# A top-k attention and low-rank mixer kernel: the softmax division moved to a tile by features, by way of DRAM

## The chip, the cores and the metric

The kernel runs on one core of a Trainium2 chip. The metric is the device time of one execution in microseconds; the median of several runs is compared. The engines named below are PE (the matrix engine; PEld is its loading of weights), DVE (vector engine), ACT (scalar engine), POOL (GpSimd) and SP (which here only issues transfers). SPq and ACTq are the queues in which SP and ACT issue transfers.

## The reference

Attention over 8 batches and 8 heads, 576 positions, 64 features a head, with only the 32 largest scores of each row kept; then a mixer that adds a low-rank mixing of the positions (rank 32) and a two-layer perceptron over the 512 features.

```python
scores = scale * np.matmul(q, k.transpose(0, 1, 3, 2))
kth = np.partition(scores, -32, axis=-1)[..., -32:-31]
scores = np.where(scores >= kth, scores, -1000000000.0)
attn = np.exp(scores - np.max(scores, axis=-1, keepdims=True))
attn = attn / (np.sum(attn, axis=-1, keepdims=True) + 1e-09)
x = heads_side_by_side(np.matmul(attn, v))        # (batch, 576, 512)
h = x.transpose(0, 2, 1) @ U @ V                  # over positions
u = x + h.transpose(0, 2, 1)
out = u + np.maximum(u @ w_ch1, 0.0) @ w_ch2
```

All data is fp32.

## The kernel before

**Pairs, tiles, steps.** Two heads make a pair g (NPAIR = 4 pairs a batch, 32 pairs). The 576 query rows of a pair are five tiles: four of 128 rows (t = 0 to 3, both heads side by side) and a tail of 64 rows (t = NT = 4, the two heads one above the other on the 128 partitions). From the second batch on (step ALONE = 20) a step handles one tile, and the fourth step of a pair handles t = 3 and the tail together. A large loop over steps n writes out by hand in which order every engine gets its work; each engine and each transfer queue runs its list strictly in that order. Step n does the scores of step n+1's tiles, the top-k search of step n, the exponentials and turned probabilities of step n-1, and the values of steps before (`weighted`).

**One tile.** PE computes the scores (`scores`, L332, L364), ACT copies them to SBUF (L377), POOL and DVE fold them (`pair`, L428 to L431), DVE searches the largest values (`front`), ACT and POOL make the probabilities, with row sums collected in `den`, one column for each tile and head. `blocks` turns the probabilities block by block on DVE (L572), stores them in DRAM (`away`, four transfers on SP, L578), and `back` fetches them in turned order (`PT<-away`, on ACT's queue, L587). The tail is turned on PE instead (`turns`).

**Values.** `values(g, t)` multiplies by V on PE. For t < NT the result lies by features: partition = head and feature, column = query row (L646, L649); ACT copies it to `XT` (L658). For the tail it lies by positions, 5 products (L633); ACT scales it with the inverse row sums from `den` into the tail part of X (L641, twice). `inverse` turns `den` into reciprocals on DVE (L621).

**Mixing.** `mixed(g, wait, lag)` is a generator, advanced once by each `fill()` of the big loop. It turns XT on PE to lie by positions (L672, four transposes), ACT copies that to X (L676), and POOL multiplies it with the inverse row sums (L677), so the division is made on the tile by positions, where a row sum belongs to a partition. Then PE multiplies with U (L688), ACT copies to Tb (L696), and in two parts (320 and 256 columns) PE multiplies with V (L700) and adds X, turned back to lie by features, into the same PSUM tile (L702: four transposes and a product with `ident2` for the tail). ACT copies the parts to `uT` (L710). Two X tiles serve the pairs in turn.

**Filler.** Each batch's perceptron (`mlp`, L742 and L760) is cut into single products, which `fill()` deals out between the steps of the next batch's attention. `turned_back` turns its results and stores them (L784 to L795). The last batch's perceptron is written out by itself after the loop (`closing`), in an order of its own.

**SP's queue** in steps of the later batches: the transfers of `away` (they wait for DVE's L572), the loads of q for the next pair in the step with t = 0 and of k and v in the step with t = 1 (`loading`, L255 to L288), and the output stores. The k and q tiles are turned by DVE (L302) a step later.

Of the kernel before, what the change touches and what calls it, by code (L numbers as in the profile page):

```python
# [8 lines left out]
F32 = mybir.dt.float32  # L9
# [3 lines left out]
ALU = mybir.AluOpType  # L13
# [13 lines left out]
def kernel(  # L27
# [28 lines left out]
    nc = tc.nc  # L56
    B, H, S, D = q.shape
    P = 128
# [37 lines left out]
    WIDE = 2 * P + TAIL  # L96

    ident = const.tile([P, P], F32, name="ident")
# [5 lines left out]
    vds = [const.tile([P, P], F32, name=f"vd{i}") for i in range(NV)]  # L104
    vts = [const.tile([P, 2, D], F32, name=f"vt{i}") for i in range(NV)]

    xs = [const.tile([P, NT + 1, P], F32, name=f"x{i}") for i in range(2)]
    for i in range(NV):
        nc.gpsimd.memset(vds[i], 0.0)
        nc.gpsimd.memset(vts[i], 0.0)  # L110
    for x in xs:
        nc.gpsimd.memset(x[:, NT, :], 0.0)
    W1Q = F // NT
    w1s = [const.tile([P, NC, W1Q], F32, name=f"w1{i}") for i in range(NT)]
    w2 = const.tile([P, NF, C], F32, name="w2")
# [2 lines left out]
    V = const.tile([NT * R, S], F32, name="V")  # L118
# [115 lines left out]

    raw, qkTs, S2s, uTs, XTs, dens = {}, {}, {}, {}, {}, {}
    probs, PTs, folds, fronts_of = {}, {}, {}, {}
    inverted, aways = set(), {}

    def load(g):

# [318 lines left out]
    def shared(g, t):  # L559


        return t < NT and g >= ROUNDED
# [29 lines left out]
    def turns(g, t):  # L592


        if shared(g, t):
            return
        E2 = probs.pop((g, t))
        nh = 2 if t < NT else 1
        if t == NT and g >= NPAIR:
            PT = attn.tile([P, NT + 1, P], F32, tag="PTt", name="PTt", bufs=1)  # L600
        else:
            PT = attn.tile([P, 2 * NT + 1, P], F32, tag="PT", name="PT")
        PTs[g, t] = PT
# [12 lines left out]

    def inverse(g, lo, hi):
        den = dens[g][:, lo:hi]
        if g == NPAIR - 1:
            nc.vector.tensor_scalar_add(den, den, 1e-9)  # L620
        nc.vector.reciprocal(den, den)  # L621

    def values(g, t):

        PT = PTs.pop((g, t))
        va, vd, vt = (a[g % NV] for a in (vas, vds, vts))
        O = ps_t.tile([P, P], F32, tag="tp", name="O")
        if t == NT:
            den, x = dens[g], xs[g % 2]
            if g not in inverted:  # L630
                inverse(g, 2 * NT if g == NPAIR - 1 else 0, 2 * NT + 1)
            for j in range(NT + 1):
                nc.tensor.matmul(  # L633
                    O,
                    lhsT=PT[:, j],
                    rhs=va[:, :, j, :] if j < NT else vt,
                    start=(j == 0),
                    stop=(j == NT),
                )
            for h in range(2):  # L640
                nc.scalar.mul(x[half(h), NT, half(h)], O[half(h), half(h)], den[half(h), 2 * NT :])  # L641
            return
        if shared(g, t):
            PT = PT.rearrange("p c n -> p (c n)")
            PT = PT.rearrange("p (a c j) -> p c a j", a=4, j=BLK)
        nc.tensor.matmul(O, lhsT=vd, rhs=PT[:, 2 * NT], start=True, stop=False)  # L646
        for j in range(NT):
            for h in range(2):
                nc.tensor.matmul(  # L649
                    O[half(h)],  # L650
                    lhsT=va[:, h, j, :],
                    rhs=PT[:, NT * h + j],
                    start=False,
                    stop=(j == NT - 1),
                )
        if t == 0:
            XTs[g] = attn.tile([P, MAIN], F32, tag="XT", name="XT", bufs=1)
        nc.scalar.copy(XTs[g][:, cols(t)], O)  # L658


    def mixed(g, wait, lag=0):

        for _ in range(lag):
            yield
        b, gi = divmod(g, NPAIR)
        if gi == 0:
            uTs[b] = mlpp.tile([P, NC, S], F32, tag="uT", name="uT")
        XT, den = XTs.pop(g), dens[g]
        X = xs[g % 2]
        tp = ps_t.tile([P, NT, P], F32, tag="tp", name="tp")  # L670
        for t in range(NT):
            nc.tensor.transpose(tp[:, t, :], XT[:, cols(t)], ident)  # L672
        X4 = X[:, 0:NT, :].rearrange("p t (h d) -> p t h d", h=2)
        tp4 = tp.rearrange("p t (h d) -> p t h d", h=2)
        den4 = den[:, 0 : 2 * NT].rearrange("p (t h) -> p t h ()", h=2).to_broadcast([P, NT, 2, D])
        nc.scalar.copy(X4, tp4)  # L676
        nc.gpsimd.tensor_tensor(X4, X4, den4, ALU.mult)  # L677
        if wait is None:
            waiting.append(g)
            while g in waiting:  # L680
                yield
        else:
            for _ in range(wait):
                yield
        pT = ps_t.tile([P, P], F32, tag="tp", name="pT")
        for t in range(NT + 1):
            i = t % NT * R
            nc.tensor.matmul(  # L688
                pT[i : i + R, :],
                lhsT=U[:, t, :],  # L690
                rhs=X[:, t, :],
                start=(t < NT),
                stop=(0 < t),
            )
        Tb = mlpp.tile([P, P], F32, tag="Tb", name="Tb")
        nc.scalar.copy(Tb, pT)  # L696
        yield
        for chunks, (lo, hi) in zip(PARTS, SPAN):
            up = ps_t.tile([P, WIDE], F32, tag="tp", name="up")
            nc.tensor.matmul(up[:, 0 : hi - lo], lhsT=Tb, rhs=V[:, lo:hi], start=True, stop=False)  # L700
            for t in chunks:
                nc.tensor.matmul(  # L702
                    up[:, OFF[t] - lo : OFF[t] - lo + rows(t)],
                    lhsT=X[:, t, :],
                    rhs=ident if t < NT else ident2,
                    is_transpose=True if t < NT else None,
                    start=False,
                    stop=(t == chunks[-1]),
                )
            nc.scalar.copy(uTs[b][:, gi, lo:hi], up[:, 0 : hi - lo])  # L710
            yield
        if gi == NPAIR - 1:
            fillers.append(closing(b) if b == B - 1 else mlp(b))
# [371 lines left out]
    def tiles(n):  # L1085

        return steps[n] if 0 <= n < STEPS else []

    def weighted(m):

        for g, t in reversed(tiles(m)):
            values(g, t)
        if tiles(m)[-1][1] == NT:
            mixing.append(mixed(g, None, 1) if m < STEPS - 1 else mixed(g, 5, 0))
# [6 lines left out]
    def turned(n):  # L1101

        for g, t in tiles(n):
            yield from turns(g, t)
# [3 lines left out]
    t = 0  # L1108
# [5 lines left out]
    for n in range(STEPS + 2):  # L1114
        if n < STEPS:
            g, t = steps[n][0]
# [6 lines left out]
        else:  # L1123
            t = NT
# [93 lines left out]
        next_params(1)  # L1218
        fill()
        if n >= STEPS:  # L1220
            weighted(n - 2)
        elif n - 2 >= ALONE and len(tiles(n - 2)) > 1:
            g2 = steps[n - 2][0][0]
            inverted.add(g2)
            inverse(g2, 0, 2 * NT + 1)
        next(here, None)
        bound = tiles(n + 1)[:1] == [(NPAIR + 1, 0)]
        if not bound:
# [7 lines left out]
        for tile_ in tiles(n - 1):  # L1236
            if shared(*tile_):
                blocks(*tile_)
        turning = turned(n - 1)
        if n < STEPS and t < 2 and g + 1 < NP:  # L1240
            if t == 0:
                coming = loading(g + 1)
            next(coming)
# [41 lines left out]
```

## Time and profile before

| | us |
|---|---|
| median of 3 runs | 1685.63 (1685.03 to 1686.02) |
| the profiled execution | 1686.28 |
| its span, first to last instruction | 1684.5 |

Over the span PE is busy 94%, the weight loads 72%, DVE 92%, ACT 59% and POOL 56%. The transfers move 180.97 MB; SP's queue carries 257712 packets and ACT's 16032. The granted clock of PE is 0.81 in the first 260 us and 0.96 to 1.00 afterwards.

| stretch, us | PE | DVE | ACT | POOL | what |
|---|---|---|---|---|---|
| 0 to 260 | 175.13 | 247.52 | 193.33 | 178.77 | first batch, parameters |
| 260 to 380 | 119.32 | 109.40 | 85.91 | 79.95 | second batch begins |
| 380 to 456.78 | 70.09 | 76.66 | 44.00 | 42.99 | |
| 836.54 to 1026.42 | 189.88 | 185.65 | 113.65 | 105.15 | one of the repeating batches |
| 1510 to 1600 | 88.05 | 42.70 | 34.43 | 42.02 | last pair, last perceptron begins |
| 1600 to 1684.5 | 80.55 | 36.19 | 12.54 | 13.54 | last perceptron |

A row gives the busy time of each engine in the stretch. An engine whose busy time equals the length of the stretch never rests there.

### The profile page before, as it was taken

The page shows a single profiled execution, that of the slowest core. Times are in us where ns is not written, and L with a number is a line of the kernel's source. Part 1 is how long each engine was busy: PE and PEld are TensorE (multiplying, and loading weights), DVE is VectorE, ACT ScalarE, POOL GpSimd, SP SyncE. Part 2 cuts the span into 40 slices and gives each one's busy share as a digit, 9 for nine tenths or more (in the row PEclk, how much of TensorE's full clock was granted, in tenths as well). Part 3 has the DMA queues.
Part 4 walks back from the last instruction along what each step waited for, and adds up shares of the span by engine and source line. Part 5 has one row for each costly group of instructions (what it writes and reads, how often), then busy time and mean ns, then how long its engine had stood idle before and what let it go on. Part 6 is the DMA issues. An engine that isn't in the chain of part 4 may idle for free.

```text
span 1684.5 us, 29512 instructions
## 1 busy us (share of the span) xinstructions
PE 1586.0 (94%) x9498; PEld 1213.4 (72%) x9498; DVE 1543.7 (92%) x4364; ACT 1000.1 (59%) x2475; POOL 939.0 (56%) x741
## 2 busy tenths in 40 slices
PE   4666799999899999999999999999999999999999
PEld 2444466788677887788777887778777887778876
DVE  7999998999999999999999999999999999994452
ACT  4888778665665656565665656565665656554320
POOL 4778668655555555555555555555555455552620
PEclk7788799999999999999999999999999999999999
DMA  3323232254545555554545555554545455533001
GB/s 87 96 75 96 58 91 73 55 133 123 131 110 136 125 131 128 131 129 120 128 117 130 125 130 125 132 125 125 128 115 131 122 134 124 131 105 102 10 1 29
DMA packets 273898, 180.97 MB, mean 107 GB/s; under 512 B 171376, under 2 KB 258256, under 8 KB 273744
## 3 DMA queue, kind: packets, MB, share of 16 engines
q1 hardware_dynamic: 257712, 117.49, 30.2%
q10 hardware_dynamic: 16032, 61.61, 11.7%
q8 instruction: 75, 1.23, 0.3%
q14 instruction: 79, 0.65, 0.1%
HBM read 108.23 MB, written 70.78 MB: 106 GB/s over the span
## 4 chain that ended last, share of the span: by engine, by line
PE 54%; DVE 32%; SPq 4%; DMA 4%; issue 2%; POOL 2%; ACT 1%; DVEq 0%; ACTq 0%; POOLq 0%
PE mm L760 16%; PE mm L742 16%; DVE m L516 10%; DVE upper L511 9%; PE sc L332 4%; PE O L649 4%; DVE first L498 3%; PE mm L836 3%; DVE y L572 3%; DVE upper L483 2%; PE sc L836 2%; PE tp L836 2%; DVE place L511 2%; DMA ld<-in_k_dram 2%; SPq L255 2%
## 5 line engine op out<-in xcount | busy, mean ns | idle before, releaser
L742 PE MATMUL mm<-uT,w 128*128 128x320 f32 (+1 forms) x1792 | 461.1, 410 | 1.9 <-ACT hT L755 1.9
L760 PE MATMUL mm<-hT,w 128*128 128x320 f32 (+1 forms) x1792 | 461.5, 408 | 0.0
L546 POOL TENSOR_TENSOR Ssb<-Ssb,E 128x576 f32<-128x576 f32 x243 | 339.4, 1416 | 210.7 <-ACT E L545 210.4
L742 PEld LDWEIGHTS mm<-uT,w 128*128 128x128 f32 x1792 | 333.7, 191 | 97.5 <-issue 12.0
L760 PEld LDWEIGHTS mm<-hT,w 128*128 128x128 f32 x1792 | 330.5, 190 | 90.3 <-issue 10.2
L516 DVE MAX8 m<-upper 128x8 f32<-128x304 f32 (+1 forms) x780 | 367.4, 512 | 0.7
L511 DVE MATCH_REPLACE8 upper<-m,upper 128x304 f32<-128x304 f32 (+1 forms) x520 | 259.9, 507 | 0.0
L431 POOL TENSOR_TENSOR lower<-lower,upper 128x576 uint32<-128x576 uint32 x108 | 152.3, 1410 | 157.5 <-DVE upper L430 152.6
L428 POOL TENSOR_TENSOR lower<-Ssb 128x576 uint32<-128x576 uint32 x108 | 152.4, 1411 | 144.0 <-ACT Ssb L377 87.0
L435 ACT ACTIVATE Ssb<-Ssb,nmax 128x576 f32<-128x576 f32 x258 | 200.8, 780 | 22.3 <-POOL Ssb L522 10.1
L332 PE MATMUL sc<-qkT 64*128 64x288 f32 (+1 forms) x1056 | 178.8, 460 | 10.8 <-ACT Ssb L386 7.8
L545 ACT ACTIVATE E<-Ssb,least 128x576 f32<-128x576 f32 x243 | 176.2, 768 | 4.2
L483 DVE MAX8 upper<-lower 128x8 f32<-128x288 f32 x432 | 172.2, 440 | 6.9 <-POOL lower L431 6.9
L377 ACT COPY Ssb<-sc 128x576 f32<-128x576 f32 x216 | 127.6, 643 | 69.2 <-PE sc L332 69.1
L572 DVE STREAM_TRANSPOSE y<-Ssb 128x512 f32<-128x512 f32 (+1 forms) x312 | 155.4, 547 | 8.8 <-ACT Ssb L435 8.8
L755 ACT ACTIVATE hT<-mm 128x320 f32<-128x320 f32 (+1 forms) x224 | 92.1, 411 | 112.2 <-PE mm L742 107.4
L649 PE MATMUL O<-PT,va 128*64 128x128 f32 x2048 | 145.1, 286 | 0.0
L332 PEld LDWEIGHTS sc<-qkT 64*128 64x128 f32 (+1 forms) x1056 | 95.7, 197 | 51.2 <-issue 16.4
L649 PEld LDWEIGHTS O<-PT,va 128*64 128x64 f32 x2048 | 113.8, 141 | 16.3 <-issue 1.6
L511 DVE MATCH_REPLACE8 upper<-first,upper 128x304 f32<-128x304 f32 x216 | 97.7, 460 | 0.0
L481 DVE MATCH_REPLACE8 lower<-upper,lower 128x288 f32<-128x288 f32 x216 | 94.1, 444 | 0.0
L430 DVE TENSOR_TENSOR upper<-sc,Ssb 128x576 f32<-128x576 f32 x108 | 80.3, 744 | 12.7 <-ACT Stail L397 12.4
(250 smaller groups left out, 2201.3 us busy)
## 6 DMA issues: line engine op xcount, KB each, us to landing
away<-y SPq DMA_DIRECT2D x416, 144.0 KB, 2.5
PT<-away ACTq DMA_DIRECT2D x104, 576.0 KB, 3.9
raw<-in_moe_w_ch_dram SPq DMA_DIRECT2D x32, 512.0 KB, 3.8
va<-in_v_dram SPq DMA_DIRECT2D x64, 128.0 KB, 2.6
out_dram<-ob SPq DMA_DIRECT2D x59, 128.0 KB, 2.5
ld<-in_q_dram SPq DMA_DIRECT2D x108, 64.0 KB, 3.1
ld<-in_k_dram SPq DMA_DIRECT2D x108, 64.0 KB, 2.6
ld<-in_q_dram SPq DMA_DIRECT2D x108, 8.0 KB, 3.2
```

The source lines that it names most:

```text
L332: nc.tensor.matmul(out, lhsT=qkT[half(h), 0, cols(t)], rhs=qkT[half(h), 1, lo:hi], start=True, stop=True,)
L428: nc.gpsimd.tensor_tensor(bottom, a.bitcast(U32), b.bitcast(U32), ALU.add)
L435: nc.scalar.activation(E, chunk, AF.Exp, bias=nmax, scale=SCALE, accum_out=total)
L483: nc.vector.max(spot, lower)
L511: nc.vector.match_replace(nxt, ms[c], curs[c], NEG)
L516: nc.vector.max(ms[c], curs[c])
L545: nc.scalar.activation(gap, chunk, AF.Relu, bias=least[:, c : c + 1], scale=-WIDEN)
L546: nc.gpsimd.tensor_tensor(chunk, chunk, gap, ALU.subtract)
L572: nc.vector.transpose(y[:, :, i * NT : i * NT + c].rearrange("p r c j -> p c r j"), E2[:, a : a + c * P].rearrange("p (c r j) -> p c r j", ...
L649: nc.tensor.matmul(O[half(h)], lhsT=va[:, h, j, :], rhs=PT[:, NT * h + j], start=False, stop=(j == NT - 1),)
L742: nc.tensor.matmul(ph[:, 0:w], lhsT=first_layer(cc, f), rhs=uT[:, cc, lo:hi], start=(cc == 0), stop=(cc == NC - 1),)
L760: nc.tensor.matmul(po[:, 0:w], lhsT=w2[:, f, c * P : (c + 1) * P], rhs=hTs[f][:, 0:w], start=(f == 0), stop=(f == NF - 1),)
```

## The change

For the pairs of the second batch on (g >= NPAIR):

- The reciprocals of all nine columns of `den` are stored, element by element, to a DRAM tile `rd` by six transfers on SP, right after `inverse`. A new `scale` fetches them, in feature order, as a row for each head, repeated over that head's 64 partitions: two transfers on SP, after `blocks` and ahead of the next pair's k loads. For the last pair both calls stand together in the step after the last.
- The tail's values are made by features too: ten products with 64 weight columns and 64 moving columns; one ACT copy into XT, which is now 576 columns wide. The two scaling copies L641 are gone here.
- `mixed` begins with a POOL product of XT (576 columns) and the scale row into `uT`, gives up its turn twice, and only then turns the result on PE (now with one transpose more, for the tail) and copies it to X (one ACT copy more). POOL's product with `den` (L677) is gone here.
- After the product with V there is no second turning of X (L702): ACT copies the product to a tile `mix` (one buffer), and POOL adds it to `uT`.

The first batch's pairs go on as before. There is one X tile in place of two, one Tb in place of two, and the tiles of a step that handles two are now taken with t = 3 first and the tail second.

```diff
-    xs = [const.tile([P, NT + 1, P], F32, name=f"x{i}") for i in range(2)]
+    X = const.tile([P, NT + 1, P], F32, name="x")
...
 def inverse(g, lo, hi):
         nc.vector.reciprocal(den, den)
+        if g >= NPAIR:
+            inverted.add(g)
+            rd = dram.tile([2, 2, WIDE], F32, tag="rd", name="rd")
+            scales[g] = rd
+            full = dens[g][:, 0 : 2 * NT].rearrange("p (a b h) -> p a b h", a=2, h=2)
+            for a in range(2):
+                for h in range(2):
+                    nc.sync.dma_start(
+                        rd[h, a, 0 : 2 * P].rearrange("(b p) -> p b", b=2), full[:, a, :, h]
+                    )
+            for h in range(2):
+                nc.sync.dma_start(
+                    rd[h, 0, 2 * P : WIDE].rearrange("(p o) -> p o", o=1), dens[g][half(h), 2 * NT :]
+                )
+
+    def scale(g):
+        rd = scales.pop(g)
+        sc = attn.tile([P, S], F32, tag="scale", name="scale", bufs=1)
+        scales[g] = sc
+        flat = rd.rearrange("h a n -> h (a n)")
+        for h in range(2):
+            nc.sync.dma_start(sc[half(h)], flat[h : h + 1, 0:S].to_broadcast([D, S]))
 
 def values(g, t):
         if t == NT:
+            if g >= NPAIR:
+                for j in range(NT + 1):
+                    for h in range(2):
+                        nc.tensor.matmul(
+                            O[half(h), 0:TAIL],
+                            lhsT=va[:, h, j, :] if j < NT else vt[:, h, :],
+                            rhs=PT[:, j, half(h)],
+                            start=(j == 0),
+                            stop=(j == NT),
+                        )
+                nc.scalar.copy(XTs[g][:, at(NT)], O[:, 0:TAIL])
+                return
...
 def mixed(g, wait, lag=0):
+        uT = uTs[b][:, gi]
+        if g >= NPAIR:
+            nc.gpsimd.tensor_tensor(uT, XT, scales.pop(g), ALU.mult)
+            yield
+            yield
+            XT = uT
         tp = ps_t.tile([P, NT, P], F32, tag="tp", name="tp")
         for t in range(NT):
-            nc.tensor.transpose(tp[:, t, :], XT[:, cols(t)], ident)
+            nc.tensor.transpose(tp[:, t, :], XT[:, at(t)], ident)
...
+        else:
+            if g == NPAIR:
+                nc.gpsimd.memset(X[TAIL:P, NT, :], 0.0)
+            tp = ps_t.tile([P, P], F32, tag="tp", name="tp")
+            nc.tensor.transpose(tp[0:TAIL], uT[:, at(NT)], ident)
+            nc.scalar.copy(X[0:TAIL, NT, :], tp[0:TAIL])
...
-            nc.tensor.matmul(up[:, 0 : hi - lo], lhsT=Tb, rhs=V[:, lo:hi], start=True, stop=False)
-            for t in chunks:
+            nc.tensor.matmul(
+                up[:, 0 : hi - lo], lhsT=Tb, rhs=V[:, lo:hi], start=True, stop=(g >= NPAIR)
+            )
+            for t in chunks if g < NPAIR else ():
...
-            nc.scalar.copy(uTs[b][:, gi, lo:hi], up[:, 0 : hi - lo])
+            if g < NPAIR:
+                nc.scalar.copy(uT[:, lo:hi], up[:, 0 : hi - lo])
+            else:
+                mix = attn.tile([P, WIDE], F32, tag="mix", name="mix", bufs=1)
+                nc.scalar.copy(mix[:, 0 : hi - lo], up[:, 0 : hi - lo])
+                nc.gpsimd.tensor_tensor(uT[:, lo:hi], uT[:, lo:hi], mix[:, 0 : hi - lo], ALU.add)
             yield
...
 def weighted(m):
-        for g, t in reversed(tiles(m)):
+        for g, t in tiles(m):
             values(g, t)
...
         if n >= STEPS:
+            if n == STEPS:
+                inverse(NP - 1, 0, 2 * NT + 1)
+                scale(NP - 1)
             weighted(n - 2)
         elif n - 2 >= ALONE and len(tiles(n - 2)) > 1:
-            g2 = steps[n - 2][0][0]
-            inverted.add(g2)
-            inverse(g2, 0, 2 * NT + 1)
+            inverse(steps[n - 2][0][0], 0, 2 * NT + 1)
...
         turning = turned(n - 1)
+        if n < STEPS and n - 2 >= ALONE and len(tiles(n - 2)) > 1:
+            scale(steps[n - 2][0][0])
         if n < STEPS and t < 2 and g + 1 < NP:
             if t == 0:
                 coming = loading(g + 1)
             next(coming)
```

More of the change, by code (lines that the diff above doesn't have):

```diff
@@ L110 @@
         nc.gpsimd.memset(vts[i], 0.0)
-    for x in xs:
-        nc.gpsimd.memset(x[:, NT, :], 0.0)
+    nc.gpsimd.memset(X[:, NT, :], 0.0)
     W1Q = F // NT
@@ L236 @@
     probs, PTs, folds, fronts_of = {}, {}, {}, {}
-    inverted, aways = set(), {}
+    inverted, aways, scales = set(), {}, {}
     def load(g):
@@ L628, in values @@
         if t == NT:
-            den, x = dens[g], xs[g % 2]
+            if g >= NPAIR:
[10 more added lines that the diff above has]
+                return
+            den = dens[g]
             if g not in inverted:
@@ L640, in values @@
             for h in range(2):
-                nc.scalar.mul(x[half(h), NT, half(h)], O[half(h), half(h)], den[half(h), 2 * NT :])
+                nc.scalar.mul(X[half(h), NT, half(h)], O[half(h), half(h)], den[half(h), 2 * NT :])
             return
@@ L656, in values @@
         if t == 0:
-            XTs[g] = attn.tile([P, MAIN], F32, tag="XT", name="XT", bufs=1)
-        nc.scalar.copy(XTs[g][:, cols(t)], O)
+            XTs[g] = attn.tile([P, S], F32, tag="XT", name="XT", bufs=1)
+        nc.scalar.copy(XTs[g][:, at(t)], O)
     def mixed(g, wait, lag=0):
@@ L668, in mixed @@
         XT, den = XTs.pop(g), dens[g]
-        X = xs[g % 2]
+        uT = uTs[b][:, gi]
[4 more added lines that the diff above has]
+            XT = uT
         tp = ps_t.tile([P, NT, P], F32, tag="tp", name="tp")
         for t in range(NT):
[L672 to L677, printed above, removed]
+            nc.tensor.transpose(tp[:, t, :], XT[:, at(t)], ident)
+        X4 = X[:, 0:NT, :]
+        nc.scalar.copy(X4, tp)
+        if g < NPAIR:
+            X4 = X4.rearrange("p t (h d) -> p t h d", h=2)
+            den4 = den[:, 0 : 2 * NT].rearrange("p (t h) -> p t h ()", h=2)
+            nc.gpsimd.tensor_tensor(X4, X4, den4.to_broadcast([P, NT, 2, D]), ALU.mult)
+        else:
[4 more added lines that the diff above has]
+            nc.scalar.copy(X[0:TAIL, NT, :], tp[0:TAIL])
         if wait is None:
@@ L694, in mixed @@
             )
-        Tb = mlpp.tile([P, P], F32, tag="Tb", name="Tb")
+        Tb = mlpp.tile([P, P], F32, tag="Tb", name="Tb", bufs=1)
         nc.scalar.copy(Tb, pT)
@@ L709, in mixed @@
                 )
-            nc.scalar.copy(uTs[b][:, gi, lo:hi], up[:, 0 : hi - lo])
+            if g < NPAIR:
+                nc.scalar.copy(uT[:, lo:hi], up[:, 0 : hi - lo])
[3 more added lines that the diff above has]
+                nc.gpsimd.tensor_tensor(uT[:, lo:hi], uT[:, lo:hi], mix[:, 0 : hi - lo], ALU.add)
             yield
```

## The prediction

> **What bounds the kernel now.** I read the table of stretches first. The batches repeat every 189.88 us from about 457 to 1406 us, so one such stretch, four head pairs of 47.47 us, stands for most of the span. In the lines below the columns are stretch, length, then busy time (and count) of PE, PEld, DVE, ACT, POOL, then clock, DMA share and GB/s.
>
> ```profile
> 646.66:836.54 189.88, 189.88 (x1169) 147.40 (x1169) 185.77 (x561) 113.53 (x286) 105.19 (x80) 1.00 0.51 127
> 1406.20:1510.00 103.80, 103.40 (x610) 77.31 (x610) 101.67 (x311) 61.85 (x157) 56.01 (x43) 1.00 0.50 125
> ```
>
> PE never rests; DVE rests 4.11 us in 189.88, about 1.03 us a pair. So time taken from PE's row of work is won, at most until DVE binds (1.03 us a pair), and every new wait of PE is lost in full. The chain of waits in that stretch is made of PE alone; these are its pieces for one pair (start, length, what; instructions counted; each fp32 product is two, each is_transpose one):
>
> ```profile
> 700.55 1.11 PE O L633 x10
> 701.89 1.02 PE O L649 x16
> 704.10 1.17 PE sc L332 x8
> 705.27 1.27 PE mm L760 x4
> 706.54 0.44 PE tp L672 x4
> 715.02 0.55 PE pT L688 x10
> 717.48 0.39 PE up L702 x4
> 719.43 0.22 PE up L702 x2
> ```
>
> The reader is to see the prices: 0.111 us for a 128-wide pass, 0.064 for a pass with 64 weight columns (L649), and 0.39 + 0.22 = 0.61 us a pair for the second turning of X (L702). The transposes L672 come 1.27 us after the scores, behind two products of L760.
>
> POOL and ACT at the same place, from the timeline:
>
> ```profile
> 704.83 1.18 ACT L377 COPY Ssb<-sc 128x576 f32<-128x576 f32 x2 [1.57 <-PE sc L332]
> 706.14 1.42 POOL L428 TENSOR_TENSOR lower<-Ssb 128x576 uint32<-128x576 uint32 x1 [1.90 <-issue]
> 708.06 1.04 POOL L677 TENSOR_TENSOR x<-x,den 128x512 f32<-128x512 f32 x1 [0.50 <-ACT x L676]
> 709.06 1.41 POOL L431 TENSOR_TENSOR lower<-lower,upper 128x576 uint32<-128x576 uint32 x1
> 723.05 1.41 POOL L431 TENSOR_TENSOR lower<-lower,upper 128x576 uint32<-128x576 uint32 x1 [3.19 <-DVE upper L430]
> ```
>
> POOL does the division after PE's transposes, and nothing of PE's waits for it soon: L688 comes at 715.02.
>
> Last, SP's queue and what DVE wants of it, same pair:
>
> ```profile
> 696.28 0.62 SPq L260 DMA_DIRECT2D ld<-in_q_dram  x1
> 698.29 0.41 SPq L790 DMA_DIRECT2D out_dram<-ob  x1
> 699.76 1.76 SPq L578 DMA_DIRECT2D away<-y  x4
> 701.57 0.59 SPq L255 DMA_DIRECT2D ld<-in_k_dram  x1
> 706.89 0.62 SPq L260 DMA_DIRECT2D ld<-in_k_dram  x1
> 711.13 1.38 DVE L302 STREAM_TRANSPOSE qkT<-ld 128x1152 f32<-128x1152 f32 x1 [0.91 <-DMA ld<-in_k_dram]
> ```
>
> SP issues without rest from the transposed blocks (699.76) to the end of the k loads (707.51), and DVE already waits 0.91 us for the last of them. In the other three pairs of the batch L302 does not wait, but starts within 4.5 us of the last k issue.
>
> **The change on PE.** Removed per pair: L702, 0.61 us. Added: one transpose of the 64 tail columns, 0.11 (a piece of L672). Changed: the tail's values, 5 products of 128 columns (1.11 us, L633), become 10 products with 64 weight columns and 64 moving ones, 20 passes. Bounds: at L649's 0.064 a pass 1.28 us, at half of it (half the moving columns) 0.64. I take 1.28, since L688, with 32 weight columns, still needs 0.055 a pass, so width buys little. Net: 0.61 - 0.11 - 0.17 = 0.33 us won a pair; with the other end 0.97. The columns t=NT-1 and t=NT only change places in one step.
>
> The Trainium skill, "TensorEngine Tiling (Array Packing)", Theoretical Speedup, gives up to 2x for 64 columns; by that the tail's values would be about 0.55 us (an estimate from 1.11) and the gain per pair 1.06. L649's row shows only 0.111/0.064 = 1.7x with 128 moving columns.
>
> **The new wait of PE.** The division now stands ahead of the transposes: POOL multiplies XT by the scale row into uT, and PE transposes uT. In POOL's order the product lies where L677 lay, between L428 and L431; in PE's order the transposes move back by two of the filler's turns, to about 2.6 to 2.8 us of products after the scores (five of 320 columns at 0.54, or six of 256 at 0.43). The chain from the scores' end (705.27): ACT's second copy ends 706.01, L428 runs 706.14 to 707.56, the product takes 1.41 (L546, same 128x576 form) and ends at 708.97. That is 3.70 us after the scores; the other three pairs give 3.70, 3.69 and 3.70 by the same rows. PE arrives after 2.7, so it waits 1.0 us (0.9 to 1.1). All it has queued (filler, next values and scores) waits with it, and ACT and DVE behind those. Nothing covers it, as PE has no idle time to move. Net on PE: +1.0 - 0.33 = +0.67 us a pair; with the other end of the values +0.03.
>
> Of the 32 pairs all but the four of the first batch change: 28. The last lies in the tail, and in the stretch 380 to 457 PE is busy 70.09 of 76.78, so I count 26: +17.4 us.
>
> **POOL and ACT.** POOL loses 1.04 (L677) and gains 1.41 + 0.87 + 0.74 (the additions at L772's 320 and 256 columns): +1.98 a pair on 26.3 of 47.47. The product ends where L677 ended (708.97 against 709.10), so L431 is not late there; the additions stand before the next L431, which waits 3.19 us for DVE: 1.61 fits. If that cover were gone, L431 and DVE's L483 would be up to 1.6 late. One buffer mix makes ACT's second copy wait for the first addition: POOL ends L428 at 719.02, so about 719.9, against 719.68 now: 0.2 us, up to 1.1 where a residual addition stands between; ACT then rests 5 us. ACT exchanges two L641 (0.61) for two copies of 0.26: nothing.
>
> **SP's queue.** Eight more issues a pair: six element-wise stores of the reciprocals, behind the q loads, and two broadcast loads between away and the k loads. Issue prices: four with 128 rows at 0.41 (L790), four with 64 rows at 0.53 (between L287's 0.51 and L795's 0.52 to 0.60): 3.76 us; bounds 0.37 to 0.64 each, 3.0 to 5.1. The stores fill SP's gap before away (2.0 to 2.9 us without the output stores, less with them) and push away by 0.65 to 1.1; the loads add 1.06. By these rows the k loads start 1.8 to 2.1 us later in all four pairs, provided the stores have landed by the end of away's issue. Stores of few bytes land in 1.4 to 2.5 us (out_dram rows), away's in 2.5: then nothing is added. At the 5.2 us that is the longest landing of ld, 2 to 3 us are added.
>
> What is late next is L302. With the k load's median landing of 2.6 us the extra stall is 0, 1.9, 0.5, 0 in the four pairs, mean 0.6; with 4.1, as in the pair shown, 1.3 to 1.9, mean 1.6. DVE has gained 0.67 of room by PE's wait, so 0 to 0.95 us a pair counts; both ends hang on whether k still meets the 576 KB of PT<-away, issued 705.48. I take 0.15 a pair, +3.9 us, near the lower end: shifted by 1.9, the last k load comes behind most of that transfer. The scale row itself lands about 705.7, 1.9 us before POOL wants it (707.56).
>
> The Trainium skill speaks against the stores: "DMA: Bandwidth & Descriptors", Rules for kernel authors, says a strided last dimension becomes one descriptor per element, and Specifications that under 512 B a read-modify-write is done. The trace shows 34155 packets on SP's queue taking 34.4% of 16 x 189.9 us, 30.6 ns each, most of 128 B; no row has 4 B ones. If the page's rule doubled that, the stores' 1152 packets (4 x 256 + 2 x 64) over 16 engines would take 4.4 instead of 2.2 us (an estimate), and the k loads some 1 to 2 us more: +26 to +50 us in all.
>
> **Start and tail.** The first four pairs keep their path. At the end the closing products start at 1570.3 and the last up ended at 1563.2; that 6.9 us of filler covers two turns and 1.6 us of additions: nothing, 2 us if the cover is gone.
>
> **Sum.** +17.4 + 3.9 = +21 on the profiled execution's 1686.28 (span 1684.5); that lies 0.65 above the median 1685.63, so 1707.
>
> **Rivals.**
> 1. *PE's gain without the wait (faster).* If the product is done when PE reaches the transposes, the 0.33 to 0.97 us a pair are kept, at most 1.03 (DVE): 28 x 0.5 = -14, 1672 (1658 to 1676). Place: PE before the transposes of uT; it decides once the wait there is below the gain. For it: POOL has 45% idle time. Against: the product stands behind L428, which hangs on the scores just computed. 0.17.
> 2. *DVE and SP bind.* With the upper end of the stall at L302, 0.95 counts instead of 0.15: 26 x (0.67 + 0.95) = +42, 1728 (1717 to 1750). For it: L302 waits already, and SP has no gap. Against: three of four pairs have room. 0.22.
> 3. *The stores are slow.* Landing after 5.2 us or more instead of 1.4 to 2.5 blocks SP, then k and POOL's product: +2.5 to 4 a pair, 1750 to 1790. For it: no row of such small pieces. Against: 4 KB stores land in 1.4 us. 0.06.
> 4. *No change.* Gain 0.97 against a wait of 1.0: 1686. 0.05.
>
> **How the numbers follow.** My forecast, 1695 to 1717, gets 0.50. This kernel's measurement can tell about 0.2% (3.4 us) from no change. Faster 0.17, same 0.05, slower 0.50 + 0.22 + 0.06 = 0.78. The range 1679 to 1750 leaves out nearly all of rival 1 and rival 3 and a little more, about 0.2.
>
> **What would show it.** The forecast: PE idle about 1 us before the transposes of uT, released by POOL, about 27 times, L702 gone in g>=4, PE busy below 100% in the stretches. Rival 2: DVE idle at L302 of over 1.5 us a pair on ld<-in_k. Rival 3: SP waiting for rd's landing, POOL's product waiting for a DMA. I am wrong if PE's wait there is under 0.4 us, or if the k loads start no later after y than now.

## The result and the profile after

| | us |
|---|---|
| before, median of 4 runs | 1685.66 (1685.03 to 1686.02) |
| after, median of 4 runs | 1969.03 (1962.33 to 1978.37) |
| ratio | 1.1685, 95% interval 1.1637 to 1.1734 |
| profiled execution after, its span | 1970.58, 1968.8 |

The change costs 283 us where 21 were forecast. First the chain that ended last in the kernel after, as shares of the span.

```profile
PE 39%; DVE 27%; DMA 23%; SPq 3%; issue 3%; ACT 2%; POOL 2%; another core or an unknown queue 0%; DVEq 0%; ACTq 0%; POOLq 0%
```

Transfers (DMA), 4% of the chain before, are 23% now. The waits of the kernel after (engine, waiting line, released by what: us in total, times, longest) say which. Line numbers are each kernel's own, so the same code has other numbers in other runs.

```profile
PE tp L711 <- POOL uT L705: 230.8, 27, 12.9
...
POOL uT L705 <- DMA scale<-rd: 163.8, 27, 11.4
...
DVE qkT L301 <- DMA ld<-in_k_dram: 120.9, 25, 5.9
...
DVE y L571 <- DMA away<-y: 74.9, 21, 8.7
```

PE waits at the place that was forecast, before the transposes of uT, and 27 times, as forecast; but 8.5 us each time instead of 1.0. Its releaser, POOL, is itself waiting for the scale tile, and DVE waits for k and for room to write the transposed blocks. All three hang on SP's queue. Its timeline for one pair (start, length of the group, line, transfer):

```profile
900.11 1.93 SPq L628 DMA_DIRECT2D rd<-den  x4
902.09 1.13 SPq L632 DMA_DIRECT2D rd<-den  x2
903.32 9.68 SPq L577 DMA_DIRECT2D away<-y  x4
913.10 1.13 SPq L643 DMA_DIRECT2D scale<-rd  x2
```

The six stores are issued in 3.1 us, near the price of 2.7. Then the four stores of the probabilities, 1.76 us before, take 9.68 us. The chain of waits at that place (start, length, what) shows what they wait for:

```profile
900.55 10.70 DMA rd<-den
...
913.68 3.18 DMA scale<-rd
...
917.00 1.41 POOL uT L705
...
918.45 1.11 PE tp L711 x4
```

A store of 256 elements, 1 KB, lands (its data is in DRAM) 10.70 us after it is issued, and the queue stands until then. The rows of SP's own waits say so too:

```profile
SPq L577 <- DMA rd<-den: 99.5, 32, 8.4
```

The loads of the scale rows follow, then POOL, then PE. Twelve such landings in the chain between 600 and 1500 us take 9.65 to 11.57 us.

Why a store of the probabilities waits for a store of something else is in the semaphores of the trace. Each transfer of SP and ACT reports its landing by one of eight semaphores, taken in turn: SP's 1453 transfers in the kernel after, and 1229 in the kernel before, never leave the turn except to skip one place for a transfer of ACT. A transfer is held until the one eight places ahead of it, which had the same semaphore, has landed. In the timeline above the third store of the probabilities is eight places behind the first store of rd.

### The profile page after: what moved, and what is told of

Same layout as the page of the kernel before. It is cut to its first block, busy times and chain, and to the rows that moved or that the text cites. A ratio compares the mean times of both kernels' runs of the same rounds, so it can differ in the third digit from the quotient of the medians.

```text
span 1968.8 us, 30218 instructions
## 1 busy us (share of the span) xinstructions
PE 1626.3 (83%) x9638; PEld 1231.7 (63%) x9638; DVE 1550.6 (79%) x4364; ACT 993.5 (50%) x2475; POOL 990.7 (50%) x797
## 4 chain that ended last, share of the span: by engine, by line
PE 39%; DVE 27%; DMA 23%; SPq 3%; issue 3%; ACT 2%; POOL 2%; another core or an unknown queue 0%; DVEq 0%; ACTq 0%; POOLq 0%
PE mm L795 12%; DMA rd<-den 12%; PE mm L813 11%; DVE m L515 8%; DVE upper L510 8%; DMA PT<-away 5%; PE O L683 3%; PE sc L331 3%; DMA scale<-rd 3%; DVE first L497 3%; PE mm L889 2%; DVE upper L482 2%; DVE y L571 2%; DMA away<-y 2%; PE tp L889 2%
## 5 line engine op out<-in xcount | busy, mean ns | idle before, releaser
L813 PE MATMUL mm<-hT,w 128*128 128x320 f32 (+1 forms) x1792 | 485.9, 423 | 0.0
L795 PE MATMUL mm<-uT,w 128*128 128x320 f32 (+1 forms) x1792 | 481.0, 423 | 2.6 <-ACT hT L808 2.2
L795 PEld LDWEIGHTS mm<-uT,w 128*128 128x128 f32 x1792 | 350.6, 200 | 108.6 <-issue 18.1
L813 PEld LDWEIGHTS mm<-hT,w 128*128 128x128 f32 x1792 | 348.5, 200 | 102.6 <-issue 19.6
L711 PE MATMUL tp<-ident,uT 128*128 128x128 f32 x112 | 29.8, 418 | 230.8 <-POOL uT L705 230.8
L711 PEld LDWEIGHTS tp<-ident,uT 128*128 128x128 f32 x112 | 19.2, 209 | 243.1 <-POOL uT L705 243.0
L301 DVE STREAM_TRANSPOSE qkT<-ld 128x1152 f32<-128x1152 f32 x27 | 37.2, 1378 | 126.2 <-DMA ld<-in_k_dram 120.9
L429 DVE TENSOR_TENSOR upper<-sc,Ssb 128x576 f32<-128x576 f32 x108 | 80.4, 744 | 65.5 <-ACT Stail L396 54.2
```

The costliest lines, as they stand in the source:

```text
L795: nc.tensor.matmul(ph[:, 0:w], lhsT=first_layer(cc, f), rhs=uT[:, cc, lo:hi], start=(cc == 0), stop=(cc == NC - 1),)
L813: nc.tensor.matmul(po[:, 0:w], lhsT=w2[:, f, c * P : (c + 1) * P], rhs=hTs[f][:, 0:w], start=(f == 0), stop=(f == NF - 1),)
```

## The experiments

Edits are against the kernel after where nothing else is said. Every time is a median; ratios are to the kernel before in the same comparison.

### Which of the four things costs: pieces, data, stores, loads

`e1_blocks`: the reciprocals are turned on DVE in 32x32 blocks first, so that four stores carry 36 pieces of 128 B in place of 1152 of 4 B; the scale tile is filled by four loads.

```diff
+            nc.vector.transpose(dT, dens32[g % 2])
+            for r in range(4):
+                nc.sync.dma_start(
+                    rd[:, r * BLK : (r + 1) * BLK], dT[r * BLK : r * BLK + 2 * NT + 1, :]
+                )
```

> The reciprocals are first turned in 32x32 blocks by DVE and stored as 36 pieces of 128 B by four transfers, in place of 1152 pieces of 4 B by six; four loads in place of two, so SP issues eight transfers a pair as in the changed kernel. Theory A (the 4 B pieces land late, about 10 us, and hold SP, POOL's product and PE): landing under 3 us, PE's wait before the transposes of uT back to 1 to 2 us, time 1690 to 1725. Theory B (eight more issues on SP are what costs): stays above 1900.

`e2_nowait`: the stores stay, the scale rows are loaded from a DRAM row that is never written again.

```diff
-        flat = rd.rearrange("h a n -> h (a n)")
+        flat = fixed
```

> The six element-wise stores stay, but the scale row is loaded from a DRAM row of ones written once at the start, so no instruction waits for the landing of the stores by its data (the output is not divided by the row sums). Theory A1 (the wait of the scale loads for the landing is what holds SP): 1700 to 1730. Theory A2 (the landing also holds SP's queue by its semaphores, which come round every eight transfers): away and k stay late, 1800 to 1930. Theory B: about 1960.

`e3_nostore`: as `e2_nowait`, and the six stores are left out.

> No stores; the two scale loads stay, from a DRAM row of ones (the output is not divided by the row sums). Theory A: 1690 to 1715. Theory B, priced by two of eight issues: 1740 to 1760.

`e4_notransfer`: neither stores nor loads; POOL multiplies by a tile of ones.

```diff
-        sc = attn.tile([P, S], F32, tag="scale", name="scale", bufs=1)
-        scales[g] = sc
+        scales[g] = ones
```

> Neither stores nor loads: POOL multiplies by a tile of ones made once (the output is not divided by the row sums). What is left is the forecast's other term, the wait of PE for POOL's product. If that wait of 1.0 us a pair against 0.33 us won is right: 1703 (1695 to 1712), PE idle about 1 us 27 times before the transposes. If the wait is hidden: 1672 (1658 to 1680).

| | median, us | range | ratio, interval |
|---|---|---|---|
| e2_nowait | 1962.61 | 1958.34 to 1972.59 | 1.1648, 1.1614 to 1.1682 |
| e1_blocks | 1772.61 | 1766.64 to 1774.58 | 1.0506, 1.0486 to 1.0527 |
| e3_nostore | 1706.32 | 1700.46 to 1709.57 | 1.0117, 1.009 to 1.0144 |
| e4_notransfer | 1681.0 | 1679.79 to 1681.34 | 0.9968, 0.9955 to 0.9981 |

Taking the data dependence away (e2) gives back 6 us only, which is within the spread of the runs: it is not that the loads need the stored values, it is the landing itself that holds the queue. The time is theory B's, but the reason is the one of theory A2, whose price was too small: SP still waits 86.4 us in 35 waits of the probabilities' stores for rd. Without the stores 256 us are gone, and without the two loads another 25. What is left, 1681.0, is the change without its transfers: 4.6 us faster than before, between the two ranges expected. The kernel with 128 B pieces kept 66 us more than that without stores, 48 above the upper end expected; most of that goes with SP's queue, as `e8_poolqueue` shows.

### Why the landing takes 10 us

`e5_half`: of the four large stores two are replaced by one row of V.

```diff
+                    if a == 1:
+                        nc.sync.dma_start(rd[h : h + 1, 1, 0 : 2 * P], V[h : h + 1, 0 : 2 * P])
+                        continue
```

> Of the four large stores of each pair the two for a=1 are replaced by one store of a row of 1 KB from V each, so that half of the 4 B pieces are gone; issues, waits and loads stay as many (the second half of the scale rows, and so the division there, is not the reference's). Theory A, the landing goes by the number of 4 B pieces (10.4 us for 1152 of them): landing 5 to 6 us, and of the 263 us between no stores (1706) and all of them (1969) about half or less goes: 1790 to 1840 us. Theory B, a fixed cost of any such store (its issue, its semaphore): landing stays above 9 us and the time above 1930 us.

Measured: 1930.22 us (1927.72 to 1945.96), ratio 1.1469, 1.1422 to 1.1516. One landing from its chain, of 8.20 to 10.92 us for the twelve between 600 and 1500 us:

```profile
946.87 10.08 DMA rd<-den
```

640 pieces land hardly sooner than 1152, so a price that goes by the number of pieces falls; the time is at the edge of theory B. Two readings are left, told apart by where the pieces fall.

`e9_apart` and `e12_apart64`: as `e2_nowait`, with the pieces 512 B and 64 B apart.

```diff
-            rd = dram.tile([2, 2, WIDE], F32, tag="rd", name="rd")
+            rd = dram.tile([2, 2, WIDE, P], F32, tag="rd", name="rd")
...
-                        rd[h, a, 0 : 2 * P].rearrange("(b p) -> p b", b=2), full[:, a, :, h]
+                        rd[h, a, 0 : 2 * P, 0].rearrange("(b p) -> p b", b=2), full[:, a, :, h]
```

> As the kernel whose scale rows come from a fixed row (1962.6; the division is left out), with the 1152 pieces of a pair written 512 B apart instead of side by side. Halving the pieces had left the landing at 8 to 11 us. Theory C, writes of 4 B that fall side by side wait for one another in the memory: apart, they land in 3 to 5 us, packets of other stores are no longer held for microseconds, and the time is 1710 to 1780 us. Theory D, each such write costs wherever it falls: landing about 10 us, 1930 to 1990 us.

> The same with the pieces 64 B apart. Theory C: if neighbours within 64 B are what collide, the time is within 15 us of the kernel with 512 B; if it is neighbours within 512 B (8 pieces in each instead of 128), it lies between that and 1962 us, nearer to the former. Theory D: 1930 to 1990 us.

Measured: 1778.41 us (1771.48 to 1780.71), ratio 1.0548, 1.0528 to 1.0567, with 512 B; 1782.84 us (1776.51 to 1784.2), ratio 1.0573, 1.0558 to 1.0589, with 64 B. The list of transfers (issues, KB each, median us from issue to landing) of the kernel with 512 B:

```profile
rd<-den SPq DMA_DIRECT2D x112, 1.0 KB, 1.7
```

and of the kernel with 64 B:

```profile
rd<-den SPq DMA_DIRECT2D x112, 1.0 KB, 1.9
```

The same 1152 pieces, the same issues: 1.7 us instead of about 10, and 184 us less, once the pieces lie apart. 64 B is enough; spacings between 4 B (side by side) and 64 B were not run, and why neighbours delay one another the records do not tell. The packet records of the trace say the same from the other side. A 4 B packet takes 9 ns (median) with and without spacing, but the longest 1152 B packet of the probabilities' stores takes 0.29 us before, 6.30 us after and 0.33 us with 512 B: other stores' packets are held up while the pieces lie side by side.

### Why 72 us are left when the stores land in 1.7 us

`e8_poolqueue`: `e1_blocks` with its four stores and four loads issued by POOL.

```diff
-                nc.sync.dma_start(
+                nc.gpsimd.dma_start(
                     rd[:, r * BLK : (r + 1) * BLK], dT[r * BLK : r * BLK + 2 * NT + 1, :]
```

> As the kernel with 36 pieces of 128 B for a pair (1772.6), with its four stores and four loads issued on POOL's queue in place of SP's. Theory A, those 67 us above the kernel without stores (1706) are SP's queue, behind whose waits the loads of k stand: DVE's wait for them goes back from 68 us to about 36 or less, and the time falls to 1690 to 1740 us. Theory B, the scale tile simply comes too late for POOL's product, whatever the queue: DVE's wait for k falls, PE's wait for the product stays at 78 us or grows, and the time stays at 1755 to 1790 us.

Measured: 1715.44 us (1712.38 to 1722.28), ratio 1.0189, 1.0164 to 1.0214; 57 us less for the same transfers. PE waits 46.2 us for POOL's product (78.6 in `e1_blocks`), DVE 11.4 us for k (68.1). Both shrink, as theory A expected, so most of it was SP's queue: the eight issues leave it, and with them their places in the turn of eight, as POOL's transfers have eight semaphores of their own.

The first idea, that the loads of k should simply come earlier, was wrong in three kernels here, and in a fourth below (`e15_poolearly`). `e13_earlyk` is `e9_apart`, `e14_earlylater` the same with later transposes, `e16_afterearly` the kernel after, each with

```diff
-            next(coming)
+            list(coming)
```

so that the loads of k and v follow those of q one step earlier.

> As the kernel with pieces 512 B apart (1778.4; scale rows from a fixed row, so the division is left out), with the loads of k and v issued one step earlier, right behind those of q, so that the stores and scale loads stand behind them on SP's queue. There DVE waits 90 us for k and PE 78 us for POOL's product. Theory Q, the 72 us above the kernel without stores are the loads of k pushed back by the issues: DVE's wait for k falls under 30 us and the time to 1705 to 1740 us. Theory R, what costs is the scale tile and the probabilities coming late behind the same issues: DVE's wait falls, the time stays at 1755 to 1785 us.

> The same, and the transposes of POOL's product two fills later. If both waits were the whole cost: PE's wait for the product falls under 25 us and the time to 1690 to 1710 us, the level of the kernel with POOL's queue (1700). If a third place binds (SP's queue itself, or the way of the probabilities through DRAM): above 1720 us.

> The change as it stands (1969.0), with the loads of k and v one step earlier. If the landing of 10 us costs mainly through the loads of k behind it: DVE's wait for k (121 us) nearly goes, and the time falls to 1840 to 1890 us. If it costs through the data of POOL's product and the stores of probabilities (PE waits 231 us for the product, DVE 75 us for the stores): 1920 to 1965 us.

Measured: 1953.3 us (ratio 1.159, 1.1571 to 1.161), 1914.91 us (1.137, 1.1347 to 1.1393) and 2134.93 us (1.2667, 1.2648 to 1.2686): 175, 136 and 166 us slower than `e9_apart`, `e9_apart` and the kernel after. For the first and the third neither expected outcome came; the second is above 1720, as expected if a third place binds. The waits of `e13_earlyk`:

```profile
POOL uT L711 <- DMA scale<-fixed: 218.2, 25, 10.3
DVE y L577 <- DMA away<-y: 146.7, 25, 7.7
```

DVE's wait for k is gone, and in its place stand the stores of the probabilities and the scale loads, now queued behind 21 loads. Here, what was moved ahead delayed what it passed.

`e17_storeslast`: `e9_apart` with the six stores issued in the same step behind the loads of k and v (the last pair's are left out).

> As the kernel with pieces 512 B apart (1778.4; the division is left out), with its six stores issued in the same step, but behind the loads of k and v instead of ahead of the stores of the probabilities: SP has as many issues, and only their place differs. Bringing the loads of k and v forward had made it slower (1953), as the stores of the probabilities then stood behind them. Theory P, it is the place on the queue, what stands ahead of the probabilities' stores and k's loads: 1705 to 1730 us, the level of the kernel without stores (1706), with DVE's wait for k down from 90 to about 40 us. Theory N, it is the number of issues or the traffic: 1760 to 1785 us.

Measured: 1712.9 us (1709.63 to 1713.67), ratio 1.0155, 1.0138 to 1.0172; 65.5 us less, as theory P expected, with the same issues but for those six. SP's timeline in `e9_apart`:

```profile
881.72 4.22 SPq L634 DMA_DIRECT2D rd<-den  x4
886.05 2.27 SPq L638 DMA_DIRECT2D rd<-den  x2
888.41 1.98 SPq L583 DMA_DIRECT2D away<-y  x4
```

and in `e17_storeslast`:

```profile
904.74 2.75 SPq L583 DMA_DIRECT2D away<-y  x4
...
908.77 0.62 SPq L260 DMA_DIRECT2D ld<-in_k_dram  x1
...
917.66 2.44 SPq L637 DMA_DIRECT2D rd<-den  x4
920.15 1.55 SPq L641 DMA_DIRECT2D rd<-den  x2
```

In the first, 6.5 us of stores stand between the loads of q and the probabilities; in the second they stand behind the loads, where the queue has its pause. Part of the 6.5 us is a wait: in the first pattern one of the six stores is often eight places behind a fetch of the probabilities, and SP waits 22.4 us in 22 waits there (2.4 us in the pair shown). How the delay reaches DVE is in the chain of waits of `e9_apart`:

```profile
889.95 2.68 DMA away<-y
...
892.81 5.45 DMA PT<-away
...
898.27 1.63 DMA ld<-in_k_dram
```

The last load of k is held until the probabilities are back (PT<-away), and these left late. Here too the turn of eight decides. Before, the transfer eight places behind this fetch is a load of v, vd (SP waits 58.7 us in 24 waits there), for which nobody waits soon. The two scale loads take the two places ahead of the fetch that loads of k had: with them on SP the eighth behind it is the last load of k (46.6 us in 24 waits in `e9_apart`, 47.1 in 24 in `e3_nostore`), for which DVE waits: 36.3 us in `e3_nostore`, 2.8 in `e4_notransfer`. In `e17_storeslast` DVE's wait for k is 43.6 us instead of 90.2 and PE's for the product 29.4 instead of 78.1.

### PE's side, and versions without SP's queue

The lines of `e4_notransfer` for one pair in the chain of waits:

```profile
888.91 0.58 PE O L638 x20
...
892.72 1.41 POOL lower L429
894.13 1.38 POOL uT L689
...
895.55 0.66 PE tp L695 x4
```

The tail's values, 1.11 us before, take 0.58 in the chain, and 0.68 from their start to the start of what follows. PE waits for the product, 0.96 us each on average (0.70 to 0.92 after 457 us), with L429 ahead of it on POOL:

```profile
PE tp L695 <- POOL uT L689: 24.9, 26, 3.8
```

`e6_later`: `e4_notransfer` with the transposes two fills later.

```diff
             nc.gpsimd.tensor_tensor(uT, XT, scales.pop(g), ALU.mult)
             yield
             yield
+            yield
+            yield
```

> As the kernel with neither stores nor loads (1681.0; POOL multiplies by ones, so the division is left out), with the transposes of the product two fills later. Theory A, the 24.9 us that PE waits before these transposes are a wait for POOL's product alone: it falls under 5 us, and the time by up to 25 us: 1657 to 1670 us, less if DVE takes over. Theory B, another wait takes its place: 1677 to 1683 us.

Measured: 1671.99 us (1669.98 to 1674.28), ratio 0.9918, 0.9903 to 0.9933. PE's wait there falls to 3.7 us, as theory A expected; of the 25 us the time gains 9, between the two ranges, and DVE is 56% of the chain (24% in `e4_notransfer`). So a change of this form, if its scale tile cost nothing, could win 0.8%.

`e7_byproduct`: the scale tile made by PE, without DRAM, and the later transposes.

```diff
+                nc.tensor.matmul(
+                    sp[half(h), t, :],
+                    lhsT=den[:, 2 * t + h : 2 * t + h + 1].to_broadcast([P, D]),
+                    rhs=ident,
```

> The scale tile is made without DRAM: ten matrix products of PE turn the reciprocals into feature layout (lhsT a reciprocal's column repeated 64 times, rhs the identity), ACT copies them, and the transposes are two fills later. Theory A (all that the change lost, it lost by the way through DRAM and by the place of the transposes): PE pays back 8 passes of 128x128 in pairs and two small ones, 0.3 to 0.6 us for a pair or 8 to 16 us, on the 1657 to 1670 of the kernel before it in this list: 1667 to 1684 us, the same or up to 1% faster than before. Theory B (scaling by features is itself dearer): above 1690 us.

Measured: 1700.63 us (1699.72 to 1701.88), ratio 1.0088, 1.0073 to 1.0103: above the range of theory A and inside that of theory B. PE's timeline shows why: the ten products are twenty passes (rows of the trace), sixteen at L631 and four at L645, and I had counted one for each. By the starts (944.98 to 946.27 us in one pair) they take 1.29 us a pair, 34 us in 26 pairs, against the 29 us between this kernel and `e6_later`. So it is PE's price for the scale tile, and nothing here says that scaling by features is itself dearer.

`e10_poollater`: `e8_poolqueue` with the later transposes. `e15_poolearly`: the same with the loads of k and v a step earlier.

> The change with 36 pieces of 128 B on POOL's queue (1715.4), and the transposes of POOL's product two fills later. If the 46 us that PE waits there are a wait for that product alone, as without transfers (where the same edit took 9 us of 1681), the time falls by 15 to 35 us: 1680 to 1700 us, no better than before by more than 0.3%. If POOL's product itself is late for the scale tile and delays what follows on POOL: 1705 to 1715 us.

> The correct change with 36 pieces of 128 B on POOL's queue and later transposes (1700.1), with the loads of k and v one step earlier. DVE's wait for k is 19 us there. If late loads of k still set its pace: 1680 to 1692 us. If POOL's own 5 us of issues for a pair do (its folds come later, DVE waits for them): 1695 to 1703 us. Below 1682 us it would beat the kernel before.

Measured: 1700.09 us (ratio 1.0093, 1.0079 to 1.0106) and 1770.44 us (1.0498, 1.0482 to 1.0514). The first gains the 15 us at the edge of what was expected; the second loses 70, and neither expected outcome came: the probabilities' stores stand behind the loads again (DVE waits 67.9 us for them).

`e11_tail`: the kernel before, with the tail's values by features alone; two small products turn them back.

```diff
+                for j in range(NT + 1):
+                    for h in range(2):
+                        nc.tensor.matmul(
+                            O[half(h), 0:TAIL],
...
+                nc.tensor.matmul(
+                    last[half(h), half(h)],
+                    lhsT=XTt[half(h)],
+                    rhs=ident[half(h), half(h)],
```

> The kernel before, with one part of the change alone: the tail's values are made by features (20 passes of 64 columns in place of 10 of 128), copied by ACT and turned by two small products; the division stays where it was and X is turned twice. PE gains 0.53 us a pair and pays some 0.13: 27 times 0.40 is 11 us; theory A, PE binds: 1672 to 1679 us; theory B, DVE or the chain at the tail's copies takes it: 1682 to 1690 us.

Measured: 1692.2 us (1691.37 to 1693.42), ratio 1.0044, 1.0031 to 1.0057: 0.4% slower, above both expected ranges, with PE busy 199.97 of 200 us in its stretches. PE's timeline for one pair:

```profile
893.11 0.69 PE L637 MATMUL O<-PTt,va 128*64 128x64 f32 x16
893.63 0.29 PE L637 MATMUL O<-PTt,vt 128*64 128x64 f32 x4
893.85 0.49 PE L660 MATMUL O<-PT,vd 128*128 128x128 f32 x2
```

From start to start the values take 0.74 us here, 0.37 less than before, but L660 behind them 0.41 instead of 0.32, and the small products 0.26: about nothing is left, and the rest of the 7 us I cannot place. Of the kernels here that compute all that the reference does, none is faster than the kernel before; the nearest of those that drop the second turning are `e10_poollater` and `e7_byproduct` with 1700.

## Why the prediction was wrong, step by step

- **What bounds the kernel.** Right: PE had no room, DVE little. With PE's load reduced and its wait gone (`e6_later`) DVE takes over after 14 us, as the 1.03 us a pair had said in kind (they would be 27 us).
- **The new wait of PE.** Right in place, cause and size where the transfers are out of the way: 1.0 forecast, 0.96 measured in `e4_notransfer`, behind the same L429, on average; from 457 us on each is 0.70 to 0.92, a little under the range of 0.9 to 1.1.
- **PE's gain.** Mis-sized. The tail's values were taken at 1.28 us, the upper bound; 0.58 was measured in the chain, 0.68 by the starts, near the lower bound of 0.64. With it the gain is 0.61 - 0.11 + 0.43 to 0.53 = 0.93 to 1.03 us a pair instead of 0.33; PE's busy time fell by 24.9 us, 0.9 a pair. That is as much as the new wait, and the change without its transfers is at -4.6 us instead of +17.4. The page "TensorEngine Tiling (Array Packing)" of the Trainium skill, Theoretical Speedup, gives up to 2x for 64 columns, by which I had estimated 0.55 for this term; the run shows 1.6x (by the starts) to 1.9x (in the chain).
- **SP's queue.** The step that failed, in two places. Its prices of issue were nearly right (2.7 us forecast for the six stores, 3.1 measured; 1.06 and 1.13 for the two loads). First, its proviso, that the stores "land in 1.4 to 2.5 us", was taken from the out_dram rows, and 10.70 was measured; the bound of 5.2 was too small as well: 184 us. Second, with landings inside my range (1.7 us, `e9_apart`) the kernel still takes 1778, not 1707: the extra stall was put at 0.15 us a pair and +3.9 us, and six stores that land in time cost 72 and the two loads 25. I had followed the delay to L302 only, pair by pair, as if the rest of the loop kept its time. The stores of the probabilities, and the load of k that waits for their return, are late too: 65.5 us hang on whether six issues stand ahead of them or behind. And the sum has no term for the places in the turn of eight, by which two more loads make the last load of k wait for the fetch of the probabilities, where a load of v had waited before.
- **The rule on small pieces.** The page "DMA: Bandwidth & Descriptors" of the Trainium skill, Specifications, has a read-modify-write under 512 B. Here 4 B pieces in 512 B blocks of their own landed in 1.7 us, and 64 B apart in 1.9, so being small does not cost the 10 us; lying side by side does. My estimate from the page, 2.2 us more, was in the right direction and far too small. Whether a read-modify-write is done here no run shows.
- **The rivals.** The third named the mechanism, SP waiting for rd and POOL's product for a transfer, and its sign in the profile came as written; its price, 2.5 to 4 us a pair, was 7 (184 us in 26 pairs) for the landing alone, and its chance of 0.06 rested on 4 KB stores that have no such pieces. The sign of the second came with it: DVE waits 4.8 us a pair for k, where over 1.5 was named.

The sum as the runs give it, in us, each the difference of two medians: the change without its transfers -4.6 (before to `e4_notransfer`), two loads on SP +25.3 (to `e3_nostore`), six stores behind everything +6.6 (to `e17_storeslast`), the same stores ahead of the probabilities +65.5 (to `e9_apart`), pieces side by side +184.2 (to `e2_nowait`), the loads' wait for the data +6.4 (to the kernel after). Together 283.4. The 6.6 and the 6.4 are no larger than the spread of single runs.

## What to carry to other kernels

A store whose elements go one by one is not priced by its bytes or its pieces but by whether its pieces fall side by side (slow at 4 B apart here, not at 64 B): measure its landing before anything is built on it. On a queue that feeds a loop, count what each new issue stands ahead of, not only how long it takes, and, where transfers share semaphores in turn, which earlier landing each one is then held for; the same six issues cost 7 or 72 us by their place. And before loads are moved forward to make room, look at what they pass.

## What the hardware showed beyond that

PE's granted clock falls in such waits, and makes each dearer than its length. The table of stretches of the kernel after, around the wait shown above (stretch, length, busy times and counts of PE, PEld, DVE, ACT, POOL, then granted clock, DMA share, GB/s):

```profile
905.00:918.00 13.00, 5.19 (x38) 3.85 (x34) 6.66 (x19) 4.13 (x12) 2.40 (x2) 0.87 0.75 98
918.00:919.80 1.80, 1.35 (x6) 1.31 (x7) 0.00 (x0) 0.20 (x1) 1.80 (x3) 0.50 0.92 189
```

When PE comes back after 8.3 us the clock is 0.50, as it is after all 25 idle times of PE of 6.0 to 12.9 us between 390 and 1780 us, and the four transposes take 1.11 us instead of 0.44. Over the span the clock is 0.902 (0.969 before, 0.967 in `e4_notransfer`), and PE is busy 1626.3 us with the 9638 passes that take 1561.1 in `e4_notransfer`: 65 us more for the same work. How much of that lies in the 283 us is not shown, as PE is not always what the others wait for. Waits of 0.70 to 0.92 us, as in `e4_notransfer`, left the clock at 1.00 in the repeating part.
